# Moving the output stores of a fused retention and MLP kernel from SyncE's queue to ScalarE's

## The chip, the cores and the metric

The kernel runs on one core of a Trainium2 chip. The metric is the device time of one execution in microseconds (us). The time before is the median of 8 runs, 300.02 us (298.19 to 300.64).

## The reference

```python
# B = H = 8, S = 576, head 64; gamma by head
scores = q @ k^T / sqrt(64)
ret    = scores * gamma ** (i - j)  where i >= j, else 0
x      = (ret @ v), heads put side by side: 4608 tokens x 512
h      = x @ w_in          # 512 -> 2048
out    = (h * cos(h)) @ w_out   # 2048 -> 512, float32
```

All inputs and the output are float32.

## The kernel before, in words

The kernel computes in bf16 and accumulates in float32. It never builds the whole score matrix: attention is done in chunks of 64 positions with a running state, `st`, in PSUM. One attention step multiplies a query chunk by the copied state (L617), adds to the state (L638), multiplies masked scores by values (L627) and forms the next scores (L608). DVE masks the scores into `pt` (L653); ACT copies the state to `sbd` and the result to `xt` (both L680).

The tokens are cut into nine bands of 512. For a band, 16 tiles of 128 hidden columns are computed (L844, four matmuls of 512 columns each for one tile). ACT takes the cosine of a tile from its PSUM bank into `cb` (L852), and DVE multiplies the bank by `cb` into `gt` (L855). Only then is the bank free again. There are six such banks, and three `cb` buffers.

The second matrix product of the first band is done plainly (L869, evicted by ACT at L881). The bands after it use one level of Strassen's scheme: seven half products (L963) on sums of token halves (DVE and POOL, L923, L928, L932) and of weight quarters. Their results pass through `sv` (ACT L1002, DVE and POOL L998) and end in one of four output buffers `os`, written by ACT (L1007) or by DVE (L998). While a Strassen band is in the second product, the next band is in the first, and attention is a band or more ahead.

Each finished `os` buffer is stored to HBM by `store`. There are 37 such buffers: 20 written by ACT, 17 by DVE. Where the 256 rows of a buffer are two whole blocks in the output, one instruction stores them (L979, 27 of them). Otherwise `store` issues one for each run of rows (L984, 22 of them): four blocks of four stores of 64 rows, four stores of 128 rows and 512 columns for the first band, and two of 128 rows and 256 columns at the very end.

SyncE (SP) issues every load of q, k and v (L433, L441, L452), the loads of `w_in`, the DMA transposes of k and q in the later part (L574, L580), and in the kernel before also the stores. "Token queue" in the name of the change is this SP queue, which carries the tokens' data. POOL issues the loads of `w_out`, casts what is loaded (L494, L522, L532) and does some sums.

The order of instructions on each engine is not written by hand. All operations are put in a list with an estimated cost, and a planner, `arrange` (L78), plays them in time steps of 0.01 us: an engine takes the first operation in its window (24 operations for PE, ACT and DVE, 6 for POOL, 4 for SP) whose inputs are there and for which a bank is free. For DMA it keeps a list per issuing queue (`rings`) with a transfer time; SP may have at most four transfers outstanding there. Operations marked `lazy` step back behind others. What comes out is a fixed order for each engine, and `emit` (L204) adds the semaphore waits. [...] So a change of a cost or a queue in one place may change the order on every engine.

Of the kernel before, what the change touches and what calls it, by code (L numbers as in the profile page):

```python
# [12 lines left out]
DM, DFF = H * D, 2048  # L13
# [45 lines left out]
class Prog:  # L59
# [18 lines left out]
    def arrange(self, filler, fill_until):  # L78
        wr, rd = {}, {}
        for n, op in enumerate(self.ops):  # L80
            op.seq, op.out, op.boxes = n, [], []
            deps = []
            for k in op.r:
                deps += wr.get(k, [])
            for k in op.w:
                deps += rd.get(k, []) + wr.get(k, [])
            for k in op.r + op.w:
                if isinstance(k, Box):
                    op.boxes.append(k)
                    k.ops.append(op)  # L90
                    k.left += 1
            for k in op.r:
                rd.setdefault(k, []).append(op)
            for k in op.w:
                wr[k], rd[k] = [op], []
            deps = list(dict.fromkeys(deps))
            op.n_in = len(deps)
            for d in deps:
                d.out.append(op)
        queue = {e: [op for op in self.ops if op.eng == e] for e in self.handle}  # L100
        free = {e: 0.75 for e in self.handle}
        free["pe"], free["act"] = 1.4, 2.1
        ready = {op: 0.0 for op in self.ops if op.n_in == 0}
        banks = list(range(self.banks - 1))
        rings = {"sp": [], "pool": []}
        done, order, now, left, lock = [], [], 0.0, len(self.ops), 0.0

        def finish(op, when):
            for x in op.out:
                x.n_in -= 1  # L110
                x.start = max(getattr(x, "start", 0.0), when)
                if x.n_in == 0:
                    ready[x] = x.start
            for b in op.boxes:
                b.left -= 1
                if b.left == 0:
                    banks.append(b.i)

        while left:
            for eng in queue:  # L120
                while free[eng] <= now:
                    pick, short = None, False
                    for op in queue[eng][:self.WINDOW[eng]]:
                        if op not in ready or ready[op] > now:
                            continue
                        want = len({b for b in op.boxes if b.i is None})
                        if want and (short or want > len(banks)):
                            short = True
                            continue
                        if op.ring and eng == "sp" and len(rings["sp"]) >= 4:  # L130
                            continue
                        if pick is None or not op.lazy:
                            pick = op
                        if not pick.lazy:
                            break
                    if pick is None:
                        if eng == "pe" and 1.4 <= now < fill_until:
                            op = Op("pe", filler, ["one", "dum"], ["fill"], None, 0.216, None)
                            op.start = now
                            order.append(op)  # L140
                            free[eng] = now + op.cost * (2 if now < SLOW else 1)
                        break
                    near = {x for x in banks if x + 1 in banks} if len(set(pick.boxes)) > 1 else set()
                    for b in pick.boxes:
                        if b.i is None:
                            b.i = next((x for x in banks if {x - 1, x + 1} & near), banks[0])
                            banks.remove(b.i)
                            near = {b.i}
                    queue[eng].remove(pick)
                    left -= 1  # L150
                    order.append(pick)
                    free[eng] = now + pick.cost * (2 if eng == "pe" and now < SLOW else 1)
                    if pick.port:
                        free[eng] += max(0.0, lock - now)
                        lock = free[eng]
                    if pick.ring:
                        rings[eng].append([pick, pick.ring, free[eng] + (0.5 if eng == "sp" else 1.5)])
                    else:
                        done.append((free[eng] + self.LAT[eng], pick))
                    if eng == "pe":  # L160
                        for x in [x for x in pick.out if x.eng == "pe"]:
                            pick.out.remove(x)
                            x.n_in -= 1
                            x.start = max(getattr(x, "start", 0.0), free[eng])
                            if x.n_in == 0:
                                ready[x] = x.start
            step = 0.01
            now = round(now + step, 4)
            if fill_until <= now < fill_until + step:
                banks.append(self.banks - 1)  # L170
            heads = [q[0] for q in rings.values() if q and q[0][2] <= now]
            for h in heads:
                h[1] -= step * h[0].pkt / sum(x[0].pkt for x in heads)
            for q in rings.values():
                if q and q[0][1] <= 0:
                    done.append((now + (1.5 if q is rings["sp"] else 2.4), q.pop(0)[0]))
            for d in [d for d in done if d[0] <= now]:
                done.remove(d)
                finish(d[1], d[0])
        tensor = [op for op in order if op.eng == "pe"]  # L180
        spare = {a for a, b in zip(tensor, tensor[1:]) if a.fn == filler != b.fn}
        self.ops = [op for op in order if op not in spare]
        self.settle()
# [102 lines left out]
def rows(s):  # L286
    t = s // 128
    uv, n = divmod(2 * t, SOLO) if t < SOLO else (t % 2, t // 2 * 2)
    if n % NR == NR - 1:
        return [(0, 64, row(uv, n)), (64, 64, row(uv, n + 1))]  # L290
    return [(0, 128, row(uv, n))]
# [7 lines left out]
def ap(t, size, p0, n, off, *dims):  # L299
    return bass.AP(t, p0 * size + off, [[size, n]] + [list(d) for d in dims])  # L300


class Kernel:
# [671 lines left out]
    def store(self, s, n, c0, cn, o):  # L975
        runs = [(x, *y) for x in range(n) for y in rows(s + 128 * x)]
        if len(runs) == 2 and n == 2 and runs[1][3] > runs[0][3]:
            gap = runs[1][3] - runs[0][3]
            self.P.add("sp", lambda e: e.dma_start(  # L979
                bass.AP(self.out, runs[0][3] * DM + c0, [[DM, 128], [gap * DM, 2], [1, cn]]),  # L980
                ap(self.OS[o], DM, 0, 128, 0, [cn, 2], [1, cn])), r=[("os", o)], sem=f"o{o}", cost=0.6, ring=0.7, pkt=0.04)
            return
        for x, p0, m, row in runs:
            self.P.add("sp", lambda e, x=x, p0=p0, m=m, row=row: e.dma_start(  # L984
                bass.AP(self.out, row * DM + c0, [[DM, m], [1, cn]]),
                ap(self.OS[o], DM, p0, m, x * cn, [1, cn])), r=[("os", o)], sem=f"o{o}", cost=0.6,
                ring=0.65 * cn / DM * m / 128, pkt=0.04)

    def strassen(self, j, last):
# [246 lines left out]
```

## Time and profile before

The profiled execution is one run of the kernel.

| | |
|---|---|
| profiled execution | 300.23 us |
| its span, first to last recorded instruction | 298.4 us |
| HBM read / written | 36.70 / 9.44 MB |
| first eviction into `os` | 63.2 us |
| first store / last store issued | 77.5 / 296.4 us |
| last DVE sum (128x256) | starts 295.94 us, 0.42 us |
| cosine L852 on ACT | 144 x 688 ns |
| product L855 on DVE | 144 x 684 ns |
| token sums on DVE, L923 and L932 | 32 x 965 ns, 32 x 1017 ns |
| store to landing, 60 to 210 us (L979 / L984) | 3.6 / 4.2 us median |
| store to landing, from 210 us (L979 / L984) | 2.2 / 2.0 us median |

In a group line the columns are: line, engine, operation, out<-in, shapes and count, then busy time and mean of one. In a line of waits, "A <- B: 7.6, 4, 3.3" says that A waited for B 7.6 us in all, 4 times, 3.3 us at the longest. In the 40 slices each digit is the busy share of 7.5 us in tenths. SPq is SP's queue of DMA instructions; the duration of a DMA instruction there is the time for which it occupies its issuing engine, not the transfer. In a timeline line the columns are start, duration, engine, line, operation, and in brackets the idle time before it and what ended it.

### The profile page before, as it was taken

Reading aid. Unit: us, or ns where it says so; the run is one execution under the profiler, and the core shown is the slowest. Engines: PE = TensorE matmul, PEld = TensorE weight load, DVE = VectorE, ACT = ScalarE, POOL = GpSimd, SP = SyncE. Lnnn points to the kernel's source line nnn. Section 1 sums busy time; section 2 is a strip of 40 time slices with the busy share of each in tenths; the row PEclk is TensorE's granted clock in tenths of the full one; section 3 lists DMA queues with packets and bytes.
Section 4 is the critical chain, followed back from the end, with each engine's and each line's share of the span. In section 5 each row is a group of like instructions: output and inputs, shape, how many; then the busy total and the mean of one; then the engine's idle time right before and its main releaser. Section 6 shows DMA issues by size and latency. Waiting matters only on the chain.

```text
span 298.4 us, 8973 instructions
## 1 busy us (share of the span) xinstructions
PE 289.0 (97%) x3763; PEld 203.7 (68%) x3763; DVE 237.9 (80%) x377; ACT 184.9 (62%) x313; POOL 166.9 (56%) x162
## 2 busy tenths in 40 slices
PE   8979899999999999999999999999999999999996
PEld 3549478865788875767576666676667676666685
DVE  5868999998899399679957996799489738964961
ACT  5338567826688276676667676766776767555511
POOL 6544572399956587186509931899275017402923
PEclk9999999999999999999999999999999999999999
DMA  7999999999999999999789997898211011102024
GB/s 202 303 335 323 277 187 207 197 243 217 230 268 154 214 269 214 152 201 191 158 160 244 216 193 198 205 163 180 56 37 54 22 35 38 55 18 70 3 70 143
DMA packets 123352, 50.00 MB, mean 168 GB/s; under 512 B 81840, under 2 KB 122800, under 8 KB 123312
## 3 DMA queue, kind: packets, MB, share of 16 engines
q1 hardware_dynamic: 121200, 47.33, 71.5%
q0 software_dynamic: 2112, 2.10, 4.4%
q8 instruction: 30, 0.49, 0.7%
q14 instruction: 10, 0.08, 0.1%
HBM read 36.70 MB, written 9.44 MB: 155 GB/s over the span
## 4 chain that ended last, share of the span: by engine, by line
PE 81%; DVE 9%; DMA 3%; SPq 3%; issue 2%; ACT 1%; DVEq 0%
PE bk L844 36%; PE bk L963 32%; PE bk L869 5%; DVE gt L855 4%; DMA gt<-in_moe_w_in_dram 3%; PE st L638 2%; PE bk L617 2%; DVE pt L712 2%; SPq L433 1%; PE bk L608 1%; PE bk L627 1%; SPq L452 1%; DVE gt L932 1%; ACT cb L852 1%; PE bk L552 1%
## 5 line engine op out<-in xcount | busy, mean ns | idle before, releaser
L844 PE MATMUL bk<-xt,win 128*128 128x512 bf16 (+2 forms) x752 | 138.0, 329 | 3.5 <-DVE pt L712 2.8
L852 ACT ACTIVATE cb<-bk,cpi 128x512 bf16<-128x512 f32 x144 | 97.9, 688 | 47.6 <-PE bk L844 45.1
L855 DVE TENSOR_TENSOR gt<-bk,cb 128x512 bf16<-128x512 f32 x144 | 95.5, 684 | 34.7 <-ACT cb L852 32.6
L844 PEld LDWEIGHTS bk<-xt,win 128*128 128x128 bf16 x752 | 70.4, 98 | 44.6 <-DVE pt L712 3.6
L998 POOL TENSOR_TENSOR sv<-sv,os 128x512 f32<-128x512 f32 x16 | 20.4, 1276 | 57.0 <-ACT os L1007 43.7
L532 POOL TENSOR_TENSOR qnat<-qstg,wt 128x512 bf16<-128x512 f32 x32 | 37.8, 1197 | 20.8 <-DMA qstg<-in_q_dram 19.0
L680 ACT ACTIVATE sbd<-st 64x512 bf16<-64x512 f32 x58 | 34.3, 592 | 13.9 <-PE bk L608 12.6
L522 POOL TENSOR_TENSOR nat<-stg,wt 128x512 bf16<-128x512 f32 x28 | 34.1, 1218 | 8.6 <-DMA stg<-in_v_dram 8.6
L494 POOL CAST nat<-stg 128x512 bf16<-128x512 f32 x36 | 26.2, 735 | 15.8 <-DMA stg<-in_k_dram 15.7
L923 DVE TENSOR_TENSOR s<-gt 128x1024 bf16<-128x1024 bf16 x32 | 30.6, 965 | 3.0 <-PE bk L963 2.8
L932 DVE TENSOR_TENSOR gt<-gt 128x1024 bf16<-128x1024 bf16 x32 | 32.5, 1017 | 0.2
L680 ACT ACTIVATE xt<-bk 128x256 bf16<-128x256 f32 (+1 forms) x64 | 26.8, 489 | 7.7 <-DVE pt L653 6.3
L963 PE MATMUL bk<-wout,gt 128*128 128x256 bf16 x256 | 31.6, 273 | 0.0
L963 PE MATMUL bk<-tw,gt 128*128 128x256 bf16 x256 | 31.3, 273 | 0.0
L963 PE MATMUL bk<-wout,s 128*128 128x256 bf16 x256 | 31.1, 273 | 0.0
L963 PEld LDWEIGHTS bk<-wout,gt 128*128 128x128 bf16 x256 | 25.0, 98 | 5.7
L928 POOL TENSOR_TENSOR s<-gt 128x512 bf16<-128x512 bf16 x16 | 23.0, 1442 | 10.4 <-DVE gt L855 10.3
L963 PEld LDWEIGHTS bk<-wout,s 128*128 128x128 bf16 x256 | 24.6, 98 | 5.7 <-DVE sv L998 0.4
L963 PEld LDWEIGHTS bk<-tw,gt 128*128 128x128 bf16 x256 | 24.2, 98 | 5.2 <-ACT sv L1002 1.0
L653 DVE TENSOR_TENSOR pt<-bk,tri 128x512 bf16<-128x512 f32 (+3 forms) x38 | 20.3, 553 | 0.6 <-PE bk L608 0.4
L1002 ACT ACTIVATE sv<-bk 128x512 f32<-128x512 f32 x16 | 9.6, 597 | 14.3 <-PE bk L963 14.1
L1007 ACT ACTIVATE os<-bk 128x512 f32<-128x512 f32 x16 | 9.6, 597 | 12.3 <-PE bk L963 12.2
(76 smaller groups left out, 284.1 us busy)
## 6 DMA issues: line engine op xcount, KB each, us to landing
out_dram<-os SPq DMA_DIRECT2D x31, 256.0 KB, 3.4
qstg<-in_q_dram SPq DMA_DIRECT2D x12, 512.0 KB, 5.7
stg<-in_k_dram SPq DMA_DIRECT2D x24, 256.0 KB, 4.1
stg<-in_v_dram SPq DMA_DIRECT2D x24, 256.0 KB, 5.0
stg<-in_k_dram SPq DMA_DIRECT2D x4, 512.0 KB, 7.6
stg<-in_v_dram SPq DMA_DIRECT2D x4, 512.0 KB, 7.5
gt<-in_moe_w_in_dram SPq DMA_DIRECT2D x4, 512.0 KB, 9.0
wout<-in_moe_w_out_dram POOLq DMA_DIRECT2D x4, 512.0 KB, 12.8
```

The source lines that it names most:

```text
L494: self.P.add(eng, lambda e: e.tensor_copy(dst, src), r=r, w=w, cost=cost, port=eng == "pool" or half == 0.75)
L522: self.P.add(eng, lambda e: e.tensor_tensor(ap(self.NAT[na], 2 * DM, 0, 128, DM, [D, H], [1, D]), ap(self.STG[st], 2 * DM, 0, 128, DM, [D, ...
L532: self.P.add(eng, lambda e, x=x: e.tensor_tensor(ap(self.QNAT[slot], 2 * DM, 0, 128, x * DM, [D, H], [1, D]), ap(self.QSTG[slot], 2 * DM, ...
L680: self.P.add(eng, (lambda e: e.activation(*io(), AF.Copy)) if eng == "act" else (lambda e: e.tensor_copy(*io())), r=r, w=w, cost=0.175 + 0 ...
L844: inst = e.matmul(self.bk(box.i, 0, 128, i * n, n), ap(self.WIN, 4 * DFF, 0, 128, c * DFF + 128 * f, [1, 128]), ap(self.XT, 4 * XR, 0, 128 ...
L852: self.P.add("act", lambda e: e.activation(ap(cb, TB, 0, 128, 0, [1, m]), self.bk(box.i, 0, 128, 0, m), AF.Sin, bias=self.CPI.ap(), scale= ...
L855: self.P.add("dve", lambda e: e.tensor_tensor(ap(gt, NF * TB, 0, 128, f0 * TB + lo - TB * j, [TB, len(fs)], [1, n]), self.half_bank(box.i, ...
L923: self.P.add("dve", lambda e: e.tensor_tensor(ap(self.S5, HF * TB, 0, 128, f * TB, [1, 2 * TB]), ap(gt, NF * TB, 0, 128, f * TB, [1, 2 * TB]),
L928: self.P.add(eng, lambda e: e.tensor_tensor(ap(self.S1, HF * HB, 0, 128, f * HB, [HB, 2], [1, HB]), half(0, 0), half(1, 1), ALU.add), r=ke ...
L932: self.P.add("dve", lambda e: e.tensor_tensor(ap(gt, NF * TB, 0, 128, f * TB + HB, [HF * TB - HB, 2], [TB, 2], [1, HB]), ap(gt, NF * TB, 0 ...
L963: inst = e.matmul(self.bk(box.i, 0, 128, at * HB, HB), ap(lt, lsize, 0, 128, loff + f * lstep + 128 * t, [1, 128]), ap(rt, rsize, 0, 128, ...
L998: self.P.add(eng, lambda e: e.tensor_tensor(out(), a(), b(), op), r=r, w=w, cost=1.2 if eng == "pool" else 0.09 + 0.00104 * n * HB, port=e ...
```

## The change

All stores in `store` are put on ACT, `nc.scalar`, in place of SP. The planner gets a third list of transfers for ACT, treats it in issue delay (0.5 us) and landing delay (1.5 us) like SP's, and counts 0.5 us of ACT's time for a store where it counted 0.6 us of SP's. The limit of four outstanding transfers stays with SP alone.

```diff
-        rings = {"sp": [], "pool": []}
+        rings = {"sp": [], "pool": [], "act": []}
...
-                        rings[eng].append([pick, pick.ring, free[eng] + (0.5 if eng == "sp" else 1.5)])
+                        rings[eng].append([pick, pick.ring, free[eng] + (1.5 if eng == "pool" else 0.5)])
...
-                    done.append((now + (1.5 if q is rings["sp"] else 2.4), q.pop(0)[0]))
+                    done.append((now + (2.4 if q is rings["pool"] else 1.5), q.pop(0)[0]))
...
         if len(runs) == 2 and n == 2 and runs[1][3] > runs[0][3]:
...
-            self.P.add("sp", lambda e: e.dma_start(
+            self.P.add("act", lambda e: e.dma_start(
...
-                ap(self.OS[o], DM, 0, 128, 0, [cn, 2], [1, cn])), r=[("os", o)], sem=f"o{o}", cost=0.6, ring=0.7, pkt=0.04)
+                ap(self.OS[o], DM, 0, 128, 0, [cn, 2], [1, cn])), r=[("os", o)], sem=f"o{o}", cost=0.5, ring=0.7, pkt=0.04)
...
         for x, p0, m, row in runs:
-            self.P.add("sp", lambda e, x=x, p0=p0, m=m, row=row: e.dma_start(
+            self.P.add("act", lambda e, x=x, p0=p0, m=m, row=row: e.dma_start(
...
-                ap(self.OS[o], DM, p0, m, x * cn, [1, cn])), r=[("os", o)], sem=f"o{o}", cost=0.6,
+                ap(self.OS[o], DM, p0, m, x * cn, [1, cn])), r=[("os", o)], sem=f"o{o}", cost=0.5,
```

The order that comes out differs on all five engines, from the second product of the first band on. SP keeps its loads and transposes.

## The prediction

> **What bounds the kernel now.** I read the page first: busy shares, then the 40 slices.
>
> ```profile
> PE 289.0 (97%) x3763; PEld 203.7 (68%) x3763; DVE 237.9 (80%) x377; ACT 184.9 (62%) x313; POOL 166.9 (56%) x162
> PE   8979899999999999999999999999999999999996
> DMA  7999999999999999999789997898211011102024
> PEclk9999999999999999999999999999999999999999
> ```
>
> TensorE is full at full clock, the DMA engines are full until about 205 us, then nearly idle. So the first question is how much idle TensorE time a different store queue could give back. The table by stretches, and who TensorE waited for from 60 us on, answer it:
>
> ```profile
> 60.00:210.00 150.00, 148.19 (x2089) 105.73 (x2088) 126.78 (x185) 99.19 (x177) 102.85 (x94) 1.00 0.99 202
> 210.00:298.40 88.40, 85.91 (x901) 60.19 (x898) 59.35 (x85) 49.41 (x83) 33.45 (x25) 1.00 0.16 51
> ...
> PE bk L617 <- issue: 0.6, 1, 0.6
> PE bk L844 <- ACT xt L680: 0.5, 1, 0.5
> PE bk L617 <- DVE gt L855: 0.3, 1, 0.3
> PE bk L844 <- DVE gt L855: 0.2, 1, 0.2
> ```
>
> The columns after the length are busy PE, PEld, DVE, ACT, POOL, then clock, DMA share, GB/s. TensorE idles 150.00 - 148.19 = 1.8 us between 60 and 210. After 210 it idles 88.40 - 85.91 = 2.5 us, which is the tail behind its last product (the final DVE sum of 0.42 us starts at 295.94, then the last store). None of its waits is on a DMA, on SP or on POOL; those named are ACT and DVE. Before 60 us it idles 60 - (289.0 - 148.2 - 85.9) = 5.1 us, but no output exists then: the first eviction into os is at 63.2 us. So the most that the middle can return is 1.8 us.
>
> **The change, part by part.** *Removed from SP: 49 store instructions.* Their durations, for 60 to 210 us (first two lines) and from 210 us (last two):
>
> ```profile
> L984 SPq DMA_DIRECT2D out_dram<-os x12: 435/630/2532, 77.5 to 138.9; - x12
> L979 SPq DMA_DIRECT2D out_dram<-os x14: 383/519/1281, 104.3 to 201.6; - x14
> ...
> L984 SPq DMA_DIRECT2D out_dram<-os x10: 350/594/597, 240.5 to 296.4; - x10
> L979 SPq DMA_DIRECT2D out_dram<-os x13: 372/373/582, 210.4 to 295.2; - x13
> ```
>
> (min/median/max ns.) From the timeline of SP, the 26 stores of the loaded stretch occupy 12.3 us (L984: 2.05, 3.24, 2.83, 4.20 for groups of 2, 2, 4, 4) plus 8.3 us (L979), 20.6 us. SP also waits 24.1 us in front of them (all rows of that kind), the longest of these:
>
> ```profile
> SPq L979 <- ACT os L1007: 7.6, 4, 3.3
> SPq L979 <- DVE os L998: 5.0, 2, 2.7
> SPq L979 <- ACT xt L680: 3.2, 1, 3.2
> ```
>
> Loads and transposes stand behind these waits, so SP gets back 20.6 + 24.1 = 44.7 us of 150. [...] Both are worth 0 us to the end: what is behind SP is POOL (23.7 us of waits for loads in this stretch), and no TensorE wait after 60 us ends on a load, a transpose or POOL. What covers the loads is the buffers staged ahead; without that cover POOL's 23.7 us is the bound, but it already exists before and reaches TensorE nowhere.
>
> *Added to ACT: the same 49 issues, in order between its evictions and cosines.* No row shows a store on ACT. Low bound: SP's prices with the DMA quiet, 0.373 for L979, 0.594 for a 64-row L984, 0.350 for a wide one. After 210: 13 x 0.373 + 8 x 0.594 + 2 x 0.350 = 10.3 us. In the loaded stretch: 14 x 0.373 + 8 x 0.594 + 4 x 0.350 = 11.4 us. High bound there: SP's measured 20.6 us. ACT then rises from 99.2 to 110.6 (or 119.8) of 150, 74% to 80%, and to 49.4 + 10.3 = 59.7 of 88. That fits as a sum; what matters is how long ACT is shut at one time, since the cosines (L852) queued behind a store feed DVE's product L855, and only that frees TensorE's bank.
>
> How much delay a bank bears: the timeline shows one turn.
>
> ```profile
> 241.45 1.03 PE L844 MATMUL bk<-xt,win 128*128 128x512 bf16 x4
> ...
> 242.51 0.69 ACT L852 ACTIVATE cb<-bk,cpi 128x512 bf16<-128x512 f32 x1 [1.05 <-PE bk L844]
> ...
> 243.30 0.69 DVE L855 TENSOR_TENSOR gt<-bk,cb 128x512 bf16<-128x512 f32 x1 [1.04 <-ACT cb L852]
> ```
>
> The bank is held from 241.45 to 243.99, 2.54 us. Of six banks I take four as turning (the Strassen sums hold about two; an estimate from the code). In a run of L844 a tile takes 0.86 us, so a bank is wanted again after 4 x 0.86 = 3.44 us: 0.9 us of slack. Where L844 alternates with L963 (0.87), it is 4 x 1.73 = 6.9 us: 4.4 us of slack. In the band from 226 to 256 us, runs of 12 and 16 matmuls hold 7 of 16 tiles, 44%. ACT adds a cover: it waits for L844 32.6 us in 79 times after 60 us, 0.4 us each.
>
> - *Single stores (27 L979, 6 wide L984).* 0.37 us, at most 1.28, against 0.9 + 0.4 = 1.3 us of cover: 0. Without cover they cost 33 x 0.37 = 12 us.
> - *Blocks of four 64-row stores.* There are four blocks, and the order of the changed kernel keeps the four in one piece on ACT. A block shuts ACT for 4 x 0.594 = 2.4 us. In a run of L844 it costs 2.4 - 1.3 = 1.1 us, elsewhere 0. Taken: 4 x 1.1 x 0.44 = 1.9 us. Bounds: 0 (all in alternation); and with SP's prices for the two early blocks (2.83, 4.20), all in runs, 1.5 + 2.9 + 2 x 1.1 = 6.6 us. I take the quiet price because on ACT's own queue no load stands in front.
> - *New waits.* 17 stores wait on ACT for a DVE sum (L998), before it only SP did, and 20 for ACT's own eviction. The own one is 0.03 us (eviction ends 291.30, store starts 291.33). The DVE ones shut ACT if DVE is late. L923 and L932 take 0.97 and 1.02 us on average where the planner counts 0.62, so a sum may come 0.4 us late: 0.4 + 0.37 is inside 1.3. Taken 0; if two long ones of 1.5 us stand ahead, 1.8 + 0.37 - 1.3 = 0.9 us, for the 14 before the last band in 44% of cases 5.5 us.
> - *The planner.* It reorders everything from the first output on: attention steps move forward by a few tiles, TensorE has the same products. Price 0, bounds -1.8 (all middle idle gone) and about +2 (as much again); 0 since those waits are on ACT and DVE, which get no lighter.
> - *Tail.* The last sum, issue (0.35) and landing (1.7) stay in series; 0, bounds 0.2 either way.
>
> [...]
>
> Sum: +1.9 us on the profiled execution of 300.23 (span 298.4 and 1.8 around it), 302.1; on the median of the runs, 300.02, it is 301.9.
>
> **The rivals.**
>
> *Faster: the cleared SP queue spreads the work.* With 44.7 us back on SP, the casts come earlier, and the planner can put attention and DVE work where DVE is free, so that the waits at 115 to 120, 144 and 167 us vanish. It pays at most 1.8 us; 0.85 of it gives 298.5. It decides if DVE's lateness there came from late loads. For it: POOL's 23.7 us. Against: the named waits are on ACT and DVE, and ACT gets more load.
>
> [...]
>
> *Hidden anyway.* All blocks fall into alternation, no gain on SP's side: 300.0. For it: 56% of the tiles are there, and ACT idles a third of the span. Against: four blocks would all have to miss. That nothing moves is excluded: the order shows all 49 on ACT.
>
> **How the numbers follow.** Blocks 0.41 (301.9), [...] hidden 0.14 (300.0), spread 0.28 (298.5). A measurement of this kernel can tell about 0.3%, 0.9 us. Hence slower 0.58, same 0.14, faster 0.28. Range: below, all middle idle gone, 300.0 - 1.8 = 298.2; above, blocks at SP's prices in runs, 300.0 + 6.6 = 306.6, cut to 306.2 as all four would have to hit. The slower cases alone span 301.0 to 306.2.
>
> **What would show it.** Right: TensorE idle between 60 us and its last product above 3 us, waits on ACT L852 or DVE L855 just behind blocks of L984 on ACT; store durations near 0.37 and 0.59; SP without waits on os; the tail unchanged at 2.5 us. [...] Wrong: TensorE idle below 1.8 us, or idle that ends on DVE work far from any store, which would be the planner's order and not the issue cost; or ACT's idle time gone without a TensorE wait.

## The result, and the profile after

| | before | after |
|---|---|---|
| median, on the same chip | 299.62 us (32 runs, 298.19 to 300.65) | 301.65 us (11 runs, 300.98 to 302.13) |
| ratio to before | | 1.0066, 95% interval 1.0053 to 1.0079 |
| profiled execution, its span | 300.23, 298.4 us | 301.51, 299.7 us |
| TensorE idle, 0 to 60 us | 5.1 us | 5.6 us |
| TensorE idle, 60 to 210 us | 1.8 us | 2.8 us |
| TensorE idle, from 210 us | 2.5 us | 2.55 us |

The change costs 2.0 us. The prediction had +1.9. The two profiled executions give only +1.3: 0.5 + 1.0 + 0.05 of idle time, less 0.3 of busy time. That of before is 0.6 us above its median and that of after 0.1 us below, so a difference of this size is read from the medians, and the traces show where some of it lies.

The page of after, its busy line and three rows of its slices (tenths of 7.5 us each):

```profile
PE 288.8 (96%) x3763; PEld 203.5 (68%) x3763; DVE 234.7 (78%) x375; ACT 183.2 (61%) x313; POOL 163.0 (54%) x162
PE   7979899999999999999989989999999999999996
PEclk9999999999999999999999999999999999999999
DMA  7999999999999899999999699545112011102024
```

The picture is that of before: TensorE full, at full clock, the same 3763 matmuls. Two new eights stand in the slices that begin near 150 and 172 us. The DMA row falls earlier, to 6 in the slice at 165 us and to 5, 4 and 5 from 187 us on, where before had 9, 8, 9 and 8, as SP, without the stores, gets ahead. The ACT row counts no store, since DMA issues are not counted as busy (x313 in both).

The stretches of after (length, then busy PE, PEld, DVE, ACT, POOL; clock, DMA share, GB/s):

```profile
60.00:210.00 150.00, 147.20 (x2080) 104.89 (x2078) 124.19 (x182) 97.38 (x176) 99.99 (x94) 1.00 1.02 203
210.00:299.70 89.70, 87.15 (x912) 61.38 (x910) 59.43 (x89) 49.55 (x84) 32.28 (x24) 1.00 0.15 49
```

And whom TensorE waited for from 60 us on:

```profile
PE bk L844 <- ACT xt L680: 1.2, 2, 0.8
PE bk L844 <- DVE gt L855: 0.9, 1, 0.9
PE bk L963 <- DVE wout L902: 0.4, 1, 0.4
```

The middle lost 150.00 - 147.20 = 2.8 us where it had lost 1.8. Two waits make 1.75 us of it. The timeline of TensorE has them at these places:

```profile
154.40 1.02 PE L844 MATMUL bk<-xt,win 128*128 128x512 bf16 x4 [0.81 <-ACT xt L680]
179.76 1.89 PE L844 MATMUL bk<-xt,win 128*128 128x512 bf16 x8 [0.94 <-DVE gt L855]
```

The stores nearest to them on ACT's queue start at 140.9 and 158.7 us for the first, 170.9 and 184.1 us for the second. Each is 0.38 us long, so none stands just ahead of either gap. Both gaps have the same pattern around them: an attention step (L617 to L608), right after it two tiles of L844, and on DVE the mask `pt` (L653) and a whole sum L932 ahead of the product L855 that would free a bank.

What the stores cost on ACT, 60 to 210 us (first two lines) and from 210 us (last two), as min/median/max ns:

```profile
L979 ACTq DMA_DIRECT2D out_dram<-os x14: 378/378/407, 104.9 to 202.2; - x14
L984 ACTq DMA_DIRECT2D out_dram<-os x12: 338/570/1043, 64.0 to 136.6; - x12
...
L979 ACTq DMA_DIRECT2D out_dram<-os x13: 378/379/382, 212.4 to 296.5; - x13
L984 ACTq DMA_DIRECT2D out_dram<-os x10: 351/608/618, 241.8 to 297.6; - x10
```

The loaded stretch has nearly the quiet price: 378 ns where SP had a median of 519, and 1043 ns at most where SP had 2532. Most stores shut ACT for the time that the prediction took.

### The profile page after: what moved, and what is told of

Its sections match the earlier page's. It is cut to its first block, busy times and chain, and to the rows that moved or that the text cites. A ratio compares the mean times of both kernels' runs of the same rounds, so it can differ in the third digit from the quotient of the medians.

```text
span 299.7 us, 8962 instructions
## 1 busy us (share of the span) xinstructions
PE 288.8 (96%) x3763; PEld 203.5 (68%) x3763; DVE 234.7 (78%) x375; ACT 183.2 (61%) x313; POOL 163.0 (54%) x162
## 4 chain that ended last, share of the span: by engine, by line
PE 77%; DMA 11%; SPq 6%; ACT 2%; DVE 1%; issue 1%; POOL 1%; DVEq 0%
PE bk L963 33%; PE bk L844 32%; DMA wout<-in_moe_w_out_dram 6%; PE bk L869 4%; SPq L466 3%; DMA stg<-in_k_dram 3%; DMA qstg<-in_q_dram 3%; SPq L433 2%; PE st L638 2%; PE bk L617 2%; PE bk L608 1%; PE bk L627 1%; ACT sbd L680 1%; DVE gt L855 1%; SPq L452 1%
## 5 line engine op out<-in xcount | busy, mean ns | idle before, releaser
L844 PE MATMUL bk<-xt,win 128*128 128x512 bf16 (+2 forms) x752 | 137.7, 329 | 5.2 <-DVE pt L712 2.8
L855 DVE TENSOR_TENSOR gt<-bk,cb 128x512 bf16<-128x512 f32 x144 | 95.5, 684 | 32.8 <-ACT cb L852 27.6
L844 PEld LDWEIGHTS bk<-xt,win 128*128 128x128 bf16 x752 | 70.4, 98 | 47.8 <-DVE pt L712 3.6
L998 POOL TENSOR_TENSOR sv<-sv,os 128x512 f32<-128x512 f32 x16 | 21.6, 1353 | 66.2 <-ACT os L1007 52.4
L532 POOL TENSOR_TENSOR qnat<-qstg,wt 128x512 bf16<-128x512 f32 x32 | 37.0, 1175 | 17.3 <-DMA qstg<-in_q_dram 17.2
L963 PE MATMUL bk<-wout,gt 128*128 128x256 bf16 x256 | 31.2, 273 | 0.4 <-DVE wout L902 0.4
L932 DVE TENSOR_TENSOR gt<-gt 128x1024 bf16<-128x1024 bf16 x32 | 31.0, 977 | 0.1
L963 PE MATMUL bk<-tw,gt 128*128 128x256 bf16 x256 | 30.8, 273 | 0.0
L963 PE MATMUL bk<-wout,s 128*128 128x256 bf16 x256 | 30.8, 273 | 0.0
L963 PEld LDWEIGHTS bk<-wout,gt 128*128 128x128 bf16 x256 | 24.9, 98 | 6.0 <-DVE wout L902 0.5
L963 PEld LDWEIGHTS bk<-wout,s 128*128 128x128 bf16 x256 | 24.6, 98 | 5.2 <-DVE sv L998 0.3
L963 PEld LDWEIGHTS bk<-tw,gt 128*128 128x128 bf16 x256 | 24.3, 98 | 4.4
L653 DVE TENSOR_TENSOR pt<-bk,tri 128x512 bf16<-128x512 f32 (+3 forms) x36 | 20.3, 579 | 6.1 <-PE bk L608 5.5
L928 POOL TENSOR_TENSOR s<-gt 128x512 bf16<-128x512 bf16 x16 | 20.5, 1288 | 5.9 <-DVE gt L855 5.9
L998 POOL TENSOR_TENSOR sv<-sv 128x512 f32<-128x512 f32 x8 | 11.9, 1490 | 14.2 <-ACT sv L1002 10.9
```

What stands on the lines that cost most here:

```text
L532: self.P.add(eng, lambda e, x=x: e.tensor_tensor(ap(self.QNAT[slot], 2 * DM, 0, 128, x * DM, [D, H], [1, D]), ap(self.QSTG[slot], 2 * DM, ...
L844: inst = e.matmul(self.bk(box.i, 0, 128, i * n, n), ap(self.WIN, 4 * DFF, 0, 128, c * DFF + 128 * f, [1, 128]), ap(self.XT, 4 * XR, 0, 128 ...
L855: self.P.add("dve", lambda e: e.tensor_tensor(ap(gt, NF * TB, 0, 128, f0 * TB + lo - TB * j, [TB, len(fs)], [1, n]), self.half_bank(box.i, ...
L928: self.P.add(eng, lambda e: e.tensor_tensor(ap(self.S1, HF * HB, 0, 128, f * HB, [HB, 2], [1, HB]), half(0, 0), half(1, 1), ALU.add), r=ke ...
L932: self.P.add("dve", lambda e: e.tensor_tensor(ap(gt, NF * TB, 0, 128, f * TB + HB, [HF * TB - HB, 2], [TB, 2], [1, HB]), ap(gt, NF * TB, 0 ...
L963: inst = e.matmul(self.bk(box.i, 0, 128, at * HB, HB), ap(lt, lsize, 0, 128, loff + f * lstep + 128 * t, [1, 128]), ap(rt, rsize, 0, 128, ...
```

## The experiments

Two theories stood for the 2.0 us. **Issue**: the stores shut ACT, above all the four blocks of four, as the prediction says. **Order**: the planner's new order makes the gaps, whatever queue the stores are on. Beside them stood the prediction's rivals (dearer issues on ACT at 304.8 us, a cleared SP queue that spreads the work). The kernels of one batch ran on one chip beside runs of the kernel before: 61 runs with median 299.73 (e1 to e4), 36 with 299.18 (e5 to e7), 51 with 299.64 (e9 to e11). All ratios are the recorded ones to those runs, with 95% intervals in brackets; they are not the quotient of the two medians, from which they differ by up to 0.2%.

### Order and queue taken apart: e1 and e2

In `before`, and in `after`, the queue of the stores is set after the planner is done. So each kernel keeps its order and has the other's queue. On TensorE the traces show it: from 180 us to the end, before and e1 have the same 996 matmuls in the same sequence, after and e2 the same 964.

```diff
 e1: before
-        self.settle()
+        [setattr(op, "eng", "act") for op in self.ops if op.sem and op.sem[0] == "o"] and self.settle()
 e2: after
-        self.settle()
+        [setattr(op, "eng", "sp") for op in self.ops if op.sem and op.sem[0] == "o"] and self.settle()
```

> The order that the planner made for the kernel before is kept on TensorE, VectorE and GpSimd; only the 49 stores are taken out of SP's stream and put into ScalarE's at the place of their planned issue. If the issues on ScalarE cost the time (issue theory), this is as slow as the changed kernel: about 301.5, ratio to before 1.005 to 1.008. If the reshuffled order costs it (order theory), this is within 0.3% of before, 299 to 300.5, with idle TensorE time between 60 and 210 us of 1.8 us as before.

> The order that the planner made for the changed kernel is kept on TensorE, VectorE and GpSimd, but the 49 stores are issued from SP, at the place of their planned issue. Issue theory: back to before, about 299.7, since no store is on ScalarE. Order theory: stays at 301 to 302, with the TensorE waits near 154 and 180 us. Against both: the stores may hold up loads on SP that this order wants early, then slower than 302.

| | order of before | order of after |
|---|---|---|
| stores on SP | 1 (before), idle 1.8 us | e2: 1.0047 [1.0030, 1.0063], idle 2.45 us |
| stores on ACT | e1: 1.0023 [1.0007, 1.0039], idle 1.7 us | after: 1.0066 [1.0053, 1.0079], idle 2.8 us |

(Idle is TensorE's between 60 and 210 us in one profiled execution.) The two effects add: 1.0047 x 1.0023 = 1.0070, and 1.0066 was measured, in another batch. So the order costs about 1.4 us (0.9 to 1.9 by the interval) and the issues about 0.6 (0.2 to 1.2 in e1). Both came out where the order theory expected them, though e1's interval leaves out 1. The trace of e2 shows the large gaps with not one store on ACT. First all its waits from 60 us on, then its timeline of TensorE:

```profile
PE bk L844 <- DVE gt L855: 1.9, 2, 0.9
PE bk L844 <- ACT xt L680: 0.4, 1, 0.4
```

```profile
154.58 1.02 PE L844 MATMUL bk<-xt,win 128*128 128x512 bf16 x4 [0.94 <-DVE gt L855]
179.94 1.89 PE L844 MATMUL bk<-xt,win 128*128 128x512 bf16 x8 [0.94 <-DVE gt L855]
```

These are the tiles of 154.40 and 179.76 in after, 0.18 us later. What released the first is named otherwise (ACT there, DVE here), but the gap is nearly the same (0.81 and 0.94 us). None of the waits ends on a DMA, on SP or on POOL, so the stores put back on SP held up nothing that TensorE wanted. In before, TensorE has no attention step right ahead of two tiles of L844 between 106 and 205 us. That is the order. It is not the whole 1.4 us: before has gaps of its own elsewhere, and this execution of e2 idles only 0.65 us more in the middle. The 0.6 us of the issues is a difference of medians only: e1 idles 1.7 us in the middle and spans 298.4 us, both as before.

### More issues in the same order: e4

After, with each paired store (L979) issued as two, one for each half: 27 more issues on ACT.

```diff
-            self.P.add("act", lambda e: e.dma_start(
...
+            self.P.add("act", lambda e: [self.P.fin(x, f"o{o}", e.dma_start(
+                bass.AP(self.out, runs[x][3] * DM + c0, [[DM, 128], [1, cn]]), ap(self.OS[o], DM, 0, 128, x * cn, [1, cn])))
+                for x in range(2)][1], r=[("os", o)], sem=f"o{o}", cost=0.5, ring=0.7, pkt=0.04).times = 2
```

> The changed kernel in its own order, with each of the 27 paired stores (L979) issued as two stores of half the size, so 27 issues of about 0.37 us more on ScalarE, 10 us. Issue theory: slower again, by 27/49 of the 1.9 us that 49 issues cost, 1.0 us or more: about 302.7. Order theory: within 0.3 us of the changed kernel, 301.4 to 302.

Measured: 302.67 us, 1.0090 [1.0054, 1.0126] (8 runs), 0.24% over after, with intervals that overlap. The 54 issues took 450 ns at the median and up to 1824, and the middle idle was 3.6 us. Taken at its middle, the ratio makes 27 more issues cost about 0.7 us, 0.03 us each, as much as all 49 did in e1. It stands where the issue theory expected it (302.7), but the overlap leaves room for no cost at all. Either way the cover that the prediction gave to single stores holds for nearly all of them.

### The block in a run of L844, as predicted: e5 and e11

After, with the store's cost in the plan at 0.0 instead of 0.5, so that the planner leaves no room for it on ACT. e11 has this order, with the stores on SP.

```diff
 e5: after, both stores
-                ... r=[("os", o)], sem=f"o{o}", cost=0.5, ring=0.7, pkt=0.04)
+                ... r=[("os", o)], sem=f"o{o}", cost=0.0, ring=0.7, pkt=0.04)
 e11: e5, and
-        self.settle()
+        [setattr(op, "eng", "sp") for op in self.ops if op.sem and op.sem[0] == "o"] and self.settle()
```

> The changed kernel, stores on ScalarE, but the planner counts 0 us of ScalarE's time for a store in place of 0.5: in its plan SP is relieved and ScalarE is not loaded. If the order got worse because SP is relieved (loads and attention pulled forward), this stays at the changed kernel's 301.5, ratio 1.005 to 1.007. If it got worse because the plan counts ScalarE's time, this falls to the kernel of before's order with stores on ScalarE: about 300.4, ratio 1.002.

> The order of the run in which the plan counts nothing on ScalarE for a store (305 us), unchanged on TensorE, VectorE and GpSimd, but the stores issued from SP. If the uncounted block of four stores on ScalarE is what makes the 2.6 us stall at 143 us and the half clock after it, both vanish and the time falls to 299.5 to 301. If that order is bad by itself, it stays above 303.

Measured: e5 305.31 us, 1.0181 [1.0149, 1.0213] (6 runs); e11 300.00 us, 1.0007 [0.9986, 1.0029] (14 runs). e11 came out as expected. For e5 neither value did (about 301.5 or 300.4). In this order the stores on ACT cost 5.3 us, and the timeline of e5 shows that one block makes most of it:

```profile
136.72 1.89 PE L844 MATMUL bk<-xt,win 128*128 128x512 bf16 x8 [0.36 <-DVE gt L932]
...
137.84 3.16 ACTq L984 DMA_DIRECT2D out_dram<-os  x4
...
141.04 1.91 PE L963 MATMUL bk<-wout,gt 128*128 128x256 bf16 x16
141.05 1.27 ACT L852 ACTIVATE cb<-bk,cpi 128x512 bf16<-128x512 f32 x2 [3.36 <-PE bk L963]
141.84 0.69 DVE L855 TENSOR_TENSOR gt<-bk,cb 128x512 bf16<-128x512 f32 x1 [2.83 <-ACT cb L852]
...
143.98 0.67 DVE L653 TENSOR_TENSOR pt<-bk,tri 128x512 bf16<-128x512 f32 x1
144.69 0.76 ACT L680 ACTIVATE xt<-bk 128x256 bf16<-128x256 f32 x2 [1.28 <-DVE pt L653]
...
145.50 4.45 PE L844 MATMUL bk<-xt,win 128*128 128x512 bf16 x12 [2.56 <-ACT xt L680]
```

The block shuts ACT from 137.84 to 141.00. The cosines start at 141.05, and DVE has stood for 2.83 us. DVE's mask `pt` comes late in turn, ACT's `xt` waits 1.28 us for it, and TensorE, which has idled 2.56 us, starts again when `xt` is out. In e11 the same block takes 2.41 us on SP, and TensorE does the same 12 matmuls without a gap ahead of them, in 2.75 us instead of 4.45:

```profile
134.74 2.41 SPq L984 DMA_DIRECT2D out_dram<-os  x4
...
138.60 1.91 PE L963 MATMUL bk<-wout,gt 128*128 128x256 bf16 x16
...
140.34 2.75 PE L844 MATMUL bk<-xt,win 128*128 128x512 bf16 x12
```

The stretches of e5 tell why they took longer (length, busy PE, PEld, DVE, ACT, POOL, the granted clock, DMA share and GB/s):

```profile
143.00:145.50 2.50, 0.00 (x0) 0.00 (x1) 2.50 (x5) 1.17 (x3) 1.04 (x1) 1.00 1.19 172
145.50:147.00 1.50, 1.50 (x4) 0.55 (x5) 1.29 (x3) 0.60 (x1) 0.00 (x0) 0.54 0.77 173
147.00:149.00 2.00, 2.00 (x6) 0.73 (x5) 0.69 (x1) 0.69 (x1) 0.61 (x1) 0.50 1.09 267
```

After the gap the granted clock is 0.54 and 0.50, until it is back at 149 us. Middle idle of 5.2 us in e5 against 1.5 in e11 is 3.7 us, and the slow clock adds 4.45 - 2.75 = 1.7 us. That is 5.4 of the 6.6 us by which the two profiled executions differ (spans of 304.3 and 297.7 us), and 2.56 + 1.7 = 4.3 us of it is the gap behind the block and the half clock after it.

Had the gap of 2.56 us cost itself alone, e5 would stand near 303.6 (an estimate: its median of 305.3 less the 1.7 us of the slow clock). The clock did not fall each time. The mean granted clock of an execution is 0.994 in three of e5's six (305.65 to 306.11 us), the profiled one among them, which is what 3.5 us at half clock make of 304. In the other three it is 1.0, and they took 302.75, 303.54 and 304.98 us, around that 303.6. So the median of 305.31 lies between two groups, and where the clock held, the stores on ACT cost about 3.5 us. What decides whether it falls is not shown: before has a mean of 0.994 in 4 of its 148 executions (299.63 to 301.13 us), without this block on ACT.

### The plan's account of a store: e3, e6, e7, e9, e10

The plan of before charges SP, that of after charges ACT. e3 changes only SP's price in before. e7 changes only ACT's price in after. e6 and e9 charge both engines and store on ACT. e10 has the order of e6 and stores on SP.

```diff
 e3: before, both stores
-                ... sem=f"o{o}", cost=0.6, ring=0.7, pkt=0.04)
+                ... sem=f"o{o}", cost=0.5, ring=0.7, pkt=0.04)
 e6: before, in arrange; stores on ACT as in e1 (e9: 0.4, 0.6)
+                    if pick.sem and pick.sem[0] == "o": free["act"] = max(free["act"], now) + 0.5
 e7: after, both stores (0.4, 0.6)
-                ... sem=f"o{o}", cost=0.5,
+                ... sem=f"o{o}", cost=0.4,
 e10: e6, but
+        [setattr(op, "eng", "sp") for op in self.ops if op.sem and op.sem[0] == "o"] and self.settle()
```

> The kernel before, stores on SP, with the planner's cost of a store changed from 0.6 to 0.5 us and nothing else: the same instructions on the same engines in a slightly different order. It measures what a reshuffle alone can do. Issue theory: within 0.2% of before. Order theory: moves by up to 0.5% either way.

> The opposite plan: a store takes 0.6 us of SP in the plan, as before, and shuts ScalarE for 0.5 us as well; the stores are then issued from ScalarE. If relieving SP makes the order worse, this is near 300.4 (ratio 1.002). If counting ScalarE's time makes it worse, this is near 301.5 (ratio 1.005 to 1.007).

> The changed kernel with 0.4 in place of 0.5 us counted for a store on ScalarE, nearer to the 0.38 measured. If the order's loss is systematic, 301 to 302 as the changed kernel. If it is chance between nearly equal plans, anywhere from 299.5 to 302.

> The changed kernel with 0.6 in place of 0.5 us counted for a store on ScalarE. Systematic: 301 to 302.3, since the plan counts still more on ScalarE. Chance between plans: anywhere from 299.5 to 302.

> The plan that loads SP with 0.6 us and ScalarE with 0.4 us for a store, stores issued from ScalarE: a second draw of that kind. If relieving SP in the plan is what makes the changed kernel's orders slower, ratio 0.998 to 1.002. If it is chance between plans, it may as well be 1.002 to 1.007.

> The plan that loads SP with 0.6 us and ScalarE with 0.6 us for a store, stores issued from ScalarE: a third draw. Relief of SP as the cause: ratio 0.998 to 1.002. Chance: may as well be 1.002 to 1.007.

> The order made with SP and ScalarE both loaded by a store (299.2 with the stores on ScalarE), unchanged on TensorE, VectorE and GpSimd, stores issued from SP. If an issue on ScalarE always costs about 0.2%, as in the first two pairs, this is 0.6 us faster, ratio 0.998 to 0.999. If the cost is nothing where the plan leaves room for the issues, the same as with ScalarE, ratio 1.000 to 1.001.

| kernel | plan charges | stores on | us (runs) | ratio [95%] | TensorE idle, 60 to 210 |
|---|---|---|---|---|---|
| e3 | SP 0.5 | SP | 299.45 (22) | 0.9982 [0.9964, 1.0001] | 1.1 |
| e7, 0.4 | ACT 0.4 | ACT | 300.05 (14) | 1.0022 [1.0005, 1.0039] | 1.6 |
| after | ACT 0.5 | ACT | 301.65 (11) | 1.0066 [1.0053, 1.0079] | 2.8 |
| e7, 0.6 | ACT 0.6 | ACT | 300.29 (15) | 1.0043 [1.0023, 1.0063] | 0.9 |
| e9, 0.4 | SP 0.6, ACT 0.4 | ACT | 299.56 (14) | 1.0002 [0.9987, 1.0017] | 1.2 |
| e6 | SP 0.6, ACT 0.5 | ACT | 299.22 (13) | 1.0006 [0.9994, 1.0018] | 0.9 |
| e9, 0.6 | SP 0.6, ACT 0.6 | ACT | 300.09 (22) | 1.0021 [1.0007, 1.0036] | 1.8 |
| e10 | order of e6 | SP | 299.23 (14) | 0.9994 [0.9977, 1.0010] | 1.3 |

What follows: a tenth of a us in one price moves the time by up to 0.4% (after against e7 at 0.4), as the order is drawn anew. So 1.4 us for the order of after is a draw among such orders, and nothing in the new queue demands it: e6 has the stores on ACT and stands at 1.0006, below both values that were expected of it. The orders that keep SP charged stand at 1.0002 to 1.0021 with ACT's stores, those that don't at 1.0022 to 1.0066. That suggests that a plan without SP's stores puts work worse, but with three orders each, and e11's order at 1.0007 without a charge on SP, it is not settled. In e6's order the stores on ACT cost 1.0006 against 0.9994 for e10: nothing that these runs tell from none. No kernel here is shown to beat before: e3 is the nearest, and its interval includes 1.

The idle column follows the time only roughly. e7 at 0.6 idles 0.9 us in its profiled execution, the shortest of its 15 (299.52 us), and yet has a median 0.4% above before. One execution does not carry differences of a us.

## Why the prediction was right, and where it was not

The time was right (301.9 predicted, 301.65 measured on a base 0.4 us lower), and so was the sign. The cause was not: the larger part came from the planner's order, and what the issues cost was not found at the blocks. Two of the signs that the prediction named for being right did not come: the middle idle stayed at 2.8 us, under 3, and its two large waits lie far from any block.

**What bounds the kernel: right.** TensorE, 1.8 us to be had in the middle. What SP was given back reached nobody: POOL's waits for loads fell from 23.7 to 16.7 us (9.0, 4.8 and 2.9), SP no longer waits on `os` and now waits on POOL's `qnat` instead (18.1 and 6.5 us for its transposes), and the last load is issued at 194.5 us instead of 202.2, with no gain on TensorE. The "spread" rival falls on this: its condition came true, the gain did not.

**Price of an issue on ACT: right.** 0.373 and 0.594 predicted, 0.378 and 0.61 measured; the paired stores kept it under load, and beside SP's own issues. Ten of the 14 in the loaded stretch began while SP was inside an issue of its own, and none took over 0.407 us. One of them:

```profile
157.63 3.31 SPq L580 DMA_TRANSPOSE qt<-qnat  x1
158.68 0.38 ACTq L979 DMA_DIRECT2D out_dram<-os  x1
```

For one block it was otherwise: that at 134.34 took 2.85 us against 2.43 in the quiet stretch, one of its stores 1.04 us, with SP issuing loads beside it (134.54 to 136.86). Whether SP's issues or the full DMA engines stretched it is not shown. The rival at 304.8 us, 0.17 of the 0.58 for slower, priced each of the two early blocks at 2.4 us, the author's estimate. It did not come: all that can be seen behind those two is 0.14 us.

**The blocks, "4 x 1.1 x 0.44 = 1.9 us": the step that failed.** The blocks are there, nearly as long as predicted, but all that can be seen of their cost to TensorE is 0.14 us. The first, from the timeline of after:

```profile
126.96 1.91 ACTq L984 DMA_DIRECT2D out_dram<-os  x3
...
128.75 1.03 PE L844 MATMUL bk<-xt,win 128*128 128x512 bf16 x4
128.91 1.27 ACT L852 ACTIVATE cb<-bk,cpi 128x512 bf16<-128x512 f32 x2 [1.90 <-PE bk L963]
129.70 0.69 DVE L855 TENSOR_TENSOR gt<-bk,cb 128x512 bf16<-128x512 f32 x1 [3.74 <-ACT cb L852]
...
130.09 0.30 PE L608 MATMUL bk<-qt,kt 64*64 64x64 bf16 x16
...
130.54 1.02 PE L844 MATMUL bk<-xt,win 128*128 128x512 bf16 x4
```

DVE stands for 3.74 us, while TensorE goes on with the next tile at 128.75 with no wait. L844 alternates with L963 there, and the 4.4 us of slack that the prediction worked out covers nearly all of it. Only the tile at 130.54 comes 0.14 us late, after DVE's product from 129.70 to 130.39; in e2, the same order without the block on ACT, it has no gap. The blocks at 241.78 and 259.79 lie in alternation too, with no gap. The one at 134.34 lies inside a run of four tiles, the case that was priced at 1.1 us:

```profile
133.14 3.62 PE L844 MATMUL bk<-xt,win 128*128 128x512 bf16 x16
134.34 2.85 ACTq L984 DMA_DIRECT2D out_dram<-os  x4
...
137.43 1.92 PE L963 MATMUL bk<-tw,gt 128*128 128x256 bf16 x16
139.19 1.04 PE L963 MATMUL bk<-wout,gt 128*128 128x256 bf16 x8
140.06 1.89 PE L844 MATMUL bk<-xt,win 128*128 128x512 bf16 x8
```

TensorE does the run without a gap. An attention step and L963 follow, and the next tile comes 2.9 us after the end of the block, when ACT has caught up. So the share was near (one block of four lay in a run), but the price failed: a run around the block cost nothing. By the comparison with e5, what counts is how soon behind the block the next tiles are due. There, with no charge on ACT in the plan, TensorE was free for a run of three tiles 1.95 us after the end of a block, and the gap and half clock behind it cost 4.3 us, more than the 1.1 us. The mechanism is real, but in the change it made 0.14 us. That the planner's charge of 0.5 us keeps blocks from such places is likely, but one order without the charge does not show it.

**Single stores, 0: nearly right.** e1, with all 49 issues, blocks included, is 0.7 us slower than before, 0.014 us a store, and in e6's order the cost is not told from zero.

**The planner, "Price 0, bounds -1.8 and about +2": wrong value, right bounds.** The order costs 1.4 us. The reason given was that the waits are on ACT and DVE, which get no lighter. That holds for gains only; it says nothing of a loss. The text did name the sign by which to tell it: idle time "that ends on DVE work far from any store, which would be the planner's order and not the issue cost". That is what the trace shows at 154 and 180 us.

**New waits and tail, 0: right.** But for the 0.14 us behind the first block, no store on ACT has a TensorE wait behind it in after. The tail is 2.5 us as before.

**What is left of the profile's +1.3 us.** 0.5 us lies before 60 us, ahead of every store, and TensorE's order first differs at 77 us. That is no effect of the change: e2 and e4, whose order is that of after, idle 6.0 and 5.0 us there, and the other kernels 4.6 to 5.7. The profiled executions show 1.0 us in the middle, the medians 2.0 us in all. The rest, nearly all of the issues' 0.6 us among it, was found in no trace, and stays open.

That the total came out right is thus partly luck: 1.9 + 0 was predicted, about 0.6 + 1.4 was measured.

## What to carry to other kernels

Where a planner orders the work, moving one operation to another queue is two changes. Freeze the order and move the queue, then take the new order with the old queue, and it shows which one pays. A DMA issue stood in ACT's stream here for 0.378 us (a paired store) or 2.4 to 3.2 us (a block of four), so charge it in the plan, and keep blocks of several issues away from the engine that frees the bottleneck's buffers, or give them a place where the bottleneck has other work: in e5 a gap and a half clock of 4.3 us stood behind one block, in after 0.14 us behind all four. No TensorE wait after 60 us ended on SP's queue, and taking the stores off it brought nothing, though SP had waited 24.1 us in front of them.

## What was not expected of the hardware

- A gap of 2.56 us in TensorE's work was followed by about 3.5 us at half clock (e5: 0.54 and 0.50 from 145.5 to 149), in the profiled execution; three of e5's six executions have the mean clock of 0.994 that goes with such a fall. The gaps of 0.94 us in after and e2 had no such effect: the clock of the stretch around them is 1.00 (after, 175 to 185 us; e2, 150 to 210 us).
- A paired store's issue took ACT 378 ns at the median at a DMA share of 1.02 (60 to 210 us, 407 at most) and of 0.15 (from 210 us, 382 at most), where the same store took SP in before 519 ns at the median and up to 1281 in the loaded stretch, among loads and transposes. With two stores in a row (e4) it stretched on ACT too, to 1824 ns at most. What stretched it is not shown.
- A store's issue on ACT ran beside an activation in flight: in after the cosine from 247.02 to 247.71 us has the store at 247.16, 0.38 us, within it, and ACT's next eviction starts at 247.73.
